# Pooled attention and a gated expert layer: batch 0's second half of k over SyncE's queue in fp32, and another order of the prologue's matmuls, copies and banks

## The chip, the cores and the metric

The kernel runs on one core of a Trainium2 chip. A core has five engines with instruction lists of their own: PE (TensorE, matrix multiplication; its weight loads are shown as PEld), DVE (VectorE), ACT (ScalarE), POOL (GpSimd) and SP (SyncE). They run side by side and wait for each other through semaphores. Data comes from HBM into SBUF by DMA. A DMA is issued by an engine, goes into that engine's queue and is worked off by 16 DMA engines that all queues share. Matmuls write into PSUM banks, and other engines copy the results from there.

The metric is the device time of one execution in microseconds, the median of several runs. Lower is better.

## The reference

```python
def _attn_ref(q, k, v) -> np.ndarray:
    B, H, S, D = q.shape          # 8, 8, 576, 64
    pool = 8
    Sp = S // pool                # 72
    scale = 1.0 / np.sqrt(D)
    k_p = k.reshape(B, H, Sp, pool, D).mean(axis=3)
    v_p = v.reshape(B, H, Sp, pool, D).mean(axis=3)
    scores = scale * np.matmul(q, k_p.transpose(0, 1, 3, 2))
    scores = scores - np.max(scores, axis=-1, keepdims=True)
    attn = np.exp(scores)
    attn = attn / (np.sum(attn, axis=-1, keepdims=True) + 1e-09)
    return np.matmul(attn, v_p).astype(np.float32)

def _moe_ref(x, w_in, w_out) -> np.ndarray:
    h = x @ w_in                  # 4608 x 512 by 512 x 2048
    g = h * np.cos(h)
    return (g @ w_out).astype(np.float32)
```

k and v are averaged over groups of eight positions, so that each head has 72 keys. The attention's output, 4608 tokens of 512 numbers, goes through two large matrix products with g = h cos(h) between them.

## The kernel before, in words

All matmuls are in bf16. The large products work on nine chunks of 512 tokens. For each chunk `up_mm` (L348) multiplies the tokens `xT` by the 16 column blocks of w_in, two blocks to a bank; ACT takes the cosine (L355), DVE multiplies (L358) and writes `g_sb`; `down_mm` (L361) multiplies by w_out and `down_out` stores the result. While PE works on chunk t, the attention of batch t + 1 is slipped between its matmuls. The attention of batch 0 has nothing to hide behind: it is the prologue, and the first L348 matmul can start only when it is done.

The order of the work is written out by hand: instructions stand on each engine in the order in which the code issues them, and an engine works its list off in order. An instruction that waits holds up everything behind it on its engine.

The prologue, by its lines:

- **Loads.** SyncE loads the first half of k (pairs of heads 0 and 1 of four) as fp32 into `k_first`, a piece of `g_sb` that is still free (L404). ACT and DVE each cast one pair to bf16 (`first_k`, L406). All other loads go over POOL's queue, which casts while it copies (`load_even`, L89): q's first half, k's second half, q's second half, v's halves, then the weights (L130, L135). Between the first two POOL computes three iotas (L413, L416), from which DVE makes `groups` (L427 to L431), the 0/1 matrix that sums groups of eight positions. POOL's later DMAs each wait for the landing of the DMA eight places ahead.
- **Warm-up.** `warm_up(n, bank)` (L472) runs n matmuls of a constant tile into a bank whose content nobody reads.
- **Pooled k.** `pool_k_mm` (L180) multiplies k by `groups`, 36 matmuls for two pairs, and hands back two closures that copy the result into `kk` (L186).
- **q transposed.** `q_transpose_mm` (L231) transposes nine blocks of q for each half; copies into `qT` follow (L232).
- **Scores.** `scores` multiplies q and pooled k (L251, eight matmuls for two units) and takes the exponential on ACT (L261) into `ex`. The list `us` has four units: token columns 0 to 255 and 256 to 511, each for heads 0 to 3 and heads 4 to 7. `REST` is the last 64 tokens for all heads.
- **Sums.** `sums_mm` (L280) sums `ex` over the keys; `inverse` makes 1/sum by Ln and Exp on ACT (L295, L296).
- **Pooled v.** `pool_v_mm` (L195), 18 matmuls for two pairs, and a copy into `vz` on DVE (L197).
- **Values.** `values_mm` (L289) multiplies `ex` by pooled v, `x_mul` (L303, DVE) multiplies by 1/sum and writes `xT`.

PSUM has three double banks (`banks[0..2]`) and two single ones (`obanks`). A step that writes a bank waits until the earlier reader of it is done, so the choice of banks is a choice of waits.

Of the kernel before, what the change touches and what calls it, by code (L numbers as in the profile page):

```python
# [9 lines left out]
FP32 = mybir.dt.float32  # L10
# [9 lines left out]
def kernel(  # L20
# [9 lines left out]
    nc = tc.nc  # L30
    B, H, S, D = q.shape
# [5 lines left out]
    KCH = d_model // 128  # L37
    FFCH = d_ff // 128
    NT = n_tokens // TILE
    ROW = S // 64  # L40
# [6 lines left out]
    REST = (SEG[2], (0, H))  # L47
# [17 lines left out]
    g_sb = wpool.tile([128, FFCH, TILE], BF16, name="g_sb")  # L65
# [11 lines left out]
    banks = [psum.tile([128, 2, 512], FP32, name=f"bank{i}") for i in range(3)]  # L77
    obanks = [psum.tile([128, 512], FP32, name=f"obank{i}") for i in range(2)]
# [6 lines left out]
    def even_view(src, b, j0=0, j1=KCH):  # L85
        return src[b, 2 * j0:2 * j1].rearrange("(j a) (p t) d -> (a p) j (t d)", a=2, t=ROW)

    def load_even(dst, b, src, j0=0, j1=KCH):
        nc.gpsimd.dma_start(out=dst[:, j0:j1].rearrange("p j t d -> p j (t d)"), in_=even_view(src, b, j0, j1))  # L89
# [100 lines left out]
    def pool_v_mm(b, pair, j0, j1):  # L190
        vb = staged["v", b]
        n = (j1 - j0) * D
        for t in range(ROW):
            for hp, rows in enumerate(half):
                nc.tensor.matmul(pair[:Sp, hp, 0:n], lhsT=groups[rows, t, :], rhs=vb[rows, j0:j1, t, :],  # L195
                                 start=(t == 0), stop=(t == ROW - 1))
        return lambda: nc.vector.tensor_copy(out=v_part(b)[:, j0:j1].rearrange("p j a d -> p a j d"),  # L197
                                             in_=pair[:Sp, :, 0:n].rearrange("p a (j d) -> p a j d", d=D))
# [26 lines left out]
    def q_transpose_mm(b, bank, g0, g1):  # L225

        if ("qT", b) not in att:
            qT_tile(b)
        ps = bank.bitcast(BF16)[:, 0:(g1 - g0) * 128].rearrange("p (g n) -> p g n", n=128)
        for g in range(g0, g1):  # L230
            nc.tensor.matmul(ps[:, g - g0, :], q_flat(b)[:, g * 128:(g + 1) * 128], identity, is_transpose=True)  # L231
        return lambda copy: copy(out=att["qT", b][:, g0:g1, :], in_=ps)  # L232
# [6 lines left out]
    def scores(b, u, pair):  # L239
        scores_mm(b, u, pair)  # L240
        scores_exp(b, u, pair)

    def scores_mm(b, u, pair):
        (c0, n), (h0, nh) = u

        for i in [i + 2 * a for k in range(0, nh, 4) for i in (k, k + 1) for a in range(2)]:
            bank, c = divmod(ex_col(u, i), nh * n // 2)
            pj, hp = divmod(h0 + i, 2)
            g, r = divmod(ROW * pj + ORDER[c0 // 64], 2)
            ps = pair[bank][:Sp, c:c + n] if isinstance(pair, tuple) else pair[:Sp, bank, c:c + n]  # L250
            nc.tensor.matmul(ps.rearrange("p (g n) -> p g n", n=64),  # L251
                             lhsT=kk[b % 2][half[r], h0 + i, 0:Sp],
                             rhs=att["qT", b][half[r], g:g + n // 64, hp * 64:hp * 64 + 64])
# [21 lines left out]
    def sums_mm(b, u, cs):  # L275

        ex = att["ex", b, u]
        q0 = u[1][0] // 4
        for i, q, rows, c in quads(u):
            nc.tensor.matmul(cs[rows, q - q0, :], lhsT=ones[:Sp, :], rhs=ex[:, c])  # L280

    def values_mm(b, u, ps):

        ex = att.pop(("ex", b, u))
        q0 = u[1][0] // 4
        for e in range(2):
            for i, q, rows, c in quads(u):
                pj, hp = divmod(u[1][0] + i, 2)
                nc.tensor.matmul(ps[rows, q - q0, e, :],  # L289
                                 lhsT=vz[b % 2][:, pj, 3 * hp, :].rearrange("p (d e) -> p e d", e=2)[:, e],  # L290
                                 rhs=ex[:, c])

    def inverse(cs, name, bufs):
        inv = asb.tile([128] + list(cs.shape[1:]), FP32, name=name, tag=name, bufs=bufs)
        nc.scalar.activation(out=inv, in_=cs, func=ACTF.Ln)  # L295
        nc.scalar.activation(out=inv, in_=inv, func=ACTF.Exp, scale=-1.0)  # L296
        return inv
# [102 lines left out]
    kv_even_tiles(0)  # L400
    q_tile(0)
    first_k = []
    k_first = g_sb.rearrange("p f n -> p (f n)").bitcast(FP32)[:, 0:2 * ROW * D]
    nc.sync.dma_start(out=k_first.rearrange("p (j n) -> p j n", j=2), in_=even_view(k, 0, 0, 2))  # L404
    for j, copy in enumerate((nc.scalar.copy, nc.vector.tensor_copy)):
        first_k.append(lambda j=j, copy=copy: copy(out=staged["k", 0][:, j].rearrange("p t d -> p (t d)"),  # L406
                                                   in_=k_first[:, j * ROW * D:(j + 1) * ROW * D]))
    first_k[0]()

    load_even(staged["q", 0], 0, q, 0, 2)  # L410
    row_of = consts.tile([128, ROW], FP32, name="row_of")
    for rows in half:
        nc.gpsimd.iota(row_of[rows], pattern=[[1, ROW]], base=0, channel_multiplier=ROW,  # L413
# [1 line left out]
    first_of = consts.tile([128, Sp], FP32, name="first_of")  # L415
    nc.gpsimd.iota(first_of, pattern=[[POOL, Sp]], base=0, channel_multiplier=0,  # L416
                   allow_small_or_imprecise_dtypes=True)
    load_even(staged["k", 0], 0, k, 2, 4)
    load_even(staged["q", 0], 0, q, 2, 4)
    load_even(staged["v", 0], 0, v, 0, 2)  # L420
    load_even(staged["v", 0], 0, v, 2, 4)
# [47 lines left out]
    def warm_up(n, bank):  # L469

        for i in range(n):
            nc.tensor.matmul(bank, lhsT=warm[:, 0:128], rhs=warm)  # L472
# [4 lines left out]
    def unit(bank):  # L477
        return bank.rearrange("p (q e n) -> p q e n", q=1, e=2)
# [2 lines left out]
    puts = pool_k_mm(0, obanks, 0, 2)  # L481
    puts[0](vec)
    puts[1](act)
    warm_up(3, banks[1][:, 0, :])
    puts = q_transpose_mm(0, banks[2][:, 0, :], 0, 5), q_transpose_mm(0, obanks[0], 5, 9)
    puts[0](vec)
    puts[1](act)
    warm_up(2, banks[1][:, 0, :])
    scores(0, us[0], banks[0])
    scores(0, us[1], banks[1])  # L490
    warm_up(1, banks[2][:, 1, :])
    for put in reversed(pool_k_mm(0, (obanks[1], obanks[0]), 2, 4)):
        put(vec)
    s01, s23 = (b_[:, 0, :].rearrange("p (i n) -> p i n", i=2) for b_ in banks[0:2])
    sums_mm(0, us[0], s01[:, 0:1])
    q_transpose_mm(0, banks[2][:, 0, :], 9, 14)(vec)
    sums_mm(0, us[1], s01[:, 1:2])
    q_transpose_mm(0, obanks[0], 14, 18)(vec)
    warm_up(1, banks[1][:, 1, :])
    inv01 = inverse(banks[0][:, 0, :], "inv", 1)  # L500
    put = pool_v_mm(0, banks[0], 0, 2)
    put()
    scores(0, us[2], banks[2])
    scores(0, us[3], banks[1])
    scores_mm(0, REST, tuple(obanks))
    for i in range(2):
        values_mm(0, us[i], unit(banks[0][:, i, :]))
    put = pool_v_mm(0, banks[2], 2, 4)
    for i in range(2):
        x_mul(0, 0, 256 * i, unit(banks[0][:, i, :]), inv01[:, 256 * i:256 * i + 256])  # L510
        if i == 0:
            put()
    for i in range(2):
        sums_mm(0, us[2 + i], s23[:, i:i + 1])
    for i in range(2):
        values_mm(0, us[2 + i], unit(banks[2][:, i, :]))
    for i in range(2):
        inv = inverse(s23[:, i, :], "inv_h", 2)
        x_mul(0, 1, 256 * i, unit(banks[2][:, i, :]), inv)
    scores_exp(0, REST, tuple(obanks))  # L520
    bk = banks
# [179 lines left out]
```

## Time and profile before

| what | value |
|---|---|
| median of 3 runs | 291.81 us (291.44 to 291.88) |
| profiled execution | 291.27 us |
| its span, first to last instruction | 289.4 us |
| PE busy | 282.8 us, 98% of the span |
| ACT / DVE / POOL busy | 142.2 / 170.0 / 146.1 us |
| first L348 matmul | at 15.97 us |
| DMA busy, first 24 us | 40 slices, nearly all at 9 tenths or more from 2.4 us on |

Times in the profile count from the first instruction. A line of the list by time has the start, the busy time, the engine, the line of code, the operation, what is written from what, the shape, the number of instructions merged into the line, and in brackets the idle time of the engine ahead of it and what ended it. The chain of waits is followed back from the last instruction: at each step to what released it.

### The profile page before, as it was taken

To read this page: it belongs to the slowest core of one execution; us is meant where nothing else is said; L and a number is where in the kernel's file an instruction comes from. 1 tells how busy PE (TensorE), PEld (TensorE's weight loads), DVE (VectorE), ACT (ScalarE), POOL (GpSimd) and SP (SyncE) were. 2 spreads that over 40 slices of the span, in tenths; PEclk is the share of its full clock that TensorE was granted. 3 is DMA by queue.
4 is the path that set the end of the run, shared out by engine and by line. 5 is a ranking of instruction groups with operands and counts; after the bars stand their busy time and mean duration, and the time that the engine had idled before them with its cause. 6 is when DMAs were issued, how large, how long until landed. Compare 5 with 4: busy or idle time off the path is not lost.

```text
span 289.4 us, 4940 instructions
## 1 busy us (share of the span) xinstructions
PE 282.8 (98%) x1993; PEld 147.3 (51%) x1993; DVE 170.0 (59%) x229; ACT 142.2 (49%) x142; POOL 146.1 (50%) x122
## 2 busy tenths in 40 slices
PE   7999999999999999999999999999999999999994
PEld 3655444555554555555555545554555454445444
DVE  5467885774757574658275737573666557216622
ACT  3786634678056904691369316840676066016400
POOL 8646937998974696479545982699000000000000
PEclk9999999999999999999999999999999999999998
DMA  7999999789977978795879866975703510230033
GB/s 142 202 204 211 205 208 197 143 164 190 167 147 102 203 114 169 101 169 110 166 74 200 120 139 119 179 139 108 140 1 73 120 39 0 49 82 16 0 72 74
DMA packets 57158, 36.59 MB, mean 126 GB/s; under 512 B 36400, under 2 KB 51184, under 8 KB 57136
## 3 DMA queue, kind: packets, MB, share of 16 engines
q0 software_dynamic: 17376, 18.06, 38.9%
q1 hardware_dynamic: 39520, 18.10, 32.3%
q8 instruction: 15, 0.25, 0.4%
q10 hardware_dynamic: 240, 0.13, 0.2%
q14 instruction: 7, 0.06, 0.1%
HBM read 36.70 MB, written 9.44 MB: 159 GB/s over the span
## 4 chain that ended last, share of the span: by engine, by line
PE 94%; DMA 2%; ACT 2%; issue 0%; DVE 0%; DVEq 0%; POOLq 0%
PE bank L348 43%; PE obank L361 27%; PE bank L361 8%; PE obank L367 5%; PE bank L251 3%; PE bank L320 3%; DMA q_b<-in_q_dram 2%; PE bank L367 2%; ACT ex L261 1%; PE bank L389 1%; PE bank L289 1%; PE bank L280 0%; PE bank L231 0%; PE obank L231 0%; PE bank L195 0%
## 5 line engine op out<-in xcount | busy, mean ns | idle before, releaser
L355 ACT ACTIVATE cos<-bank,half_pi 128x1024 f32<-128x1024 f32 x72 | 80.4, 1118 | 115.4 <-PE bank L348 115.4
L348 PE MATMUL bank<-xT,w_in_sb 128*128 128x512 bf16 x576 | 126.1, 379 | 0.0
L358 DVE TENSOR_TENSOR g_sb<-bank,cos 128x1024 bf16<-128x1024 f32 x72 | 88.1, 1224 | 48.9 <-ACT cos L355 48.8
L348 PEld LDWEIGHTS <-w_in_sb 128*128 128x128 bf16 x576 | 65.1, 113 | 59.2 <-issue 0.4
L361 PE MATMUL obank<-w_out_sb,g_sb 128*128 128x512 bf16 x360 | 83.9, 379 | 0.0
L361 PEld LDWEIGHTS <-g_sb 128*128 128x128 bf16 x462 | 42.0, 97 | 45.9 <-issue 2.0
L161 POOL TENSOR_TENSOR kv_st<-kv_st 72x2048 f32<-72x2048 bf16 (+1 forms) x13 | 50.4, 3875 | 16.9 <-DMA kv_st<-in_k_dram 16.8
L374 DVE COPY o_sb<-obank 128x512 f32<-128x512 f32 x21 | 14.4, 690 | 31.5 <-PE obank L361 28.6
L261 ACT ACTIVATE ex<-bank 72x1024 bf16<-72x1024 f32 x32 | 30.4, 1019 | 5.0 <-PE bank L251 5.0
L164 POOL TENSOR_TENSOR kv_st<-kv_st 72x1024 f32<-72x1024 f32 (+1 forms) x13 | 29.3, 2252 | 0.9
L361 PE MATMUL bank<-w_out_sb,g_sb 128*128 128x512 bf16 x102 | 27.6, 379 | 0.0
L324 DVE TENSOR_TENSOR x_r<-bank,inv_r 128x512 bf16<-128x512 f32 (+1 forms) x32 | 22.0, 689 | 1.1
L367 PE MATMUL obank<-w_out_sb,g_sb 64*128 64x512 bf16 x144 | 18.3, 376 | 0.0
L168 POOL TENSOR_TENSOR kp<-kv_st 72x512 bf16<-72x512 f32 (+1 forms) x14 | 16.1, 1169 | 0.5
L367 PEld LDWEIGHTS <-g_sb 64*128 64x128 bf16 x196 | 9.8, 94 | 7.3
L251 PE MATMUL bank<-qT,kk 64*72 64x256 bf16 (+1 forms) x184 | 13.2, 250 | 0.2
L251 PEld LDWEIGHTS <-kk 64*72 64x72 bf16 x192 | 8.4, 111 | 7.9 <-issue 3.4
L119 POOL DMA_DIRECT2D kv_st<-in_v_dram x15 | 9.7, 657 | 4.6 <-DVE vz L171 4.3
L320 PEld LDWEIGHTS <-ex 72*128 72x128 bf16 x192 | 8.7, 97 | 6.2 <-ACT ex L261 1.7
L321 DVE RECIPROCAL inv_r<-bank 128x8 f32<-128x8 f32 (+1 forms) x32 | 6.5, 203 | 8.2 <-PE bank L320 7.5
L529 POOL COPY gate<-kk 1x1 bf16<-1x1 bf16 x5 | 0.9, 178 | 20.4 <-DMA kk<-kp 20.4
L376 DVE COPY o_sb<-obank 128x512 f32<-128x512 f32 x6 | 4.1, 691 | 11.9 <-PE obank L367 11.9
(79 smaller groups left out, 167.3 us busy)
## 6 DMA issues: line engine op xcount, KB each, us to landing
out_dram<-o_sb SPq DMA_DIRECT2D x70, 128.0 KB, 2.4
q_b<-in_q_dram POOLq DMA_DIRECT2D x6, 576.0 KB, 8.8
kv_st<-in_k_dram POOLq DMA_DIRECT2D x6, 512.0 KB, 6.2
kv_st<-in_v_dram POOLq DMA_DIRECT2D x6, 512.0 KB, 10.1
w_in_sb<-in_moe_w_in_dram POOLq DMA_DIRECT2D x8, 256.0 KB, 10.8
w_out_sb<-in_moe_w_out_dram POOLq DMA_DIRECT2D x8, 256.0 KB, 10.0
q_b<-in_q_dram POOLq DMA_DIRECT2D x4, 288.0 KB, 8.4
kv_st<-in_k_dram POOLq DMA_DIRECT2D x3, 288.0 KB, 9.7
```

Of the source, the lines that this page charges most:

```text
L161: add(out=s, in0=x[:, :, 0:4, :], in1=x[:, :, 4:8, :], op=ADD)
L164: add(out=s[:, :, 0:2, :], in0=s[:, :, 0:2, :], in1=s[:, :, 2:4, :], op=ADD)
L168: add(out=kp[:, h0:h1, slot, :], in0=s[:, :, 0, :], in1=s[:, :, 1, :], op=ADD)
L251: nc.tensor.matmul(ps.rearrange("p (g n) -> p g n", n=64), lhsT=kk[b % 2][half[r], h0 + i, 0:Sp], rhs=att["qT", b][half[r], g:g + n // 64, ...
L261: nc.scalar.activation(out=ex[:, c:c + m * w].rearrange("p (a n) -> p a n", a=m), in_=src, func=ACTF.Exp, scale=scale / POOL)
L320: nc.tensor.matmul(out[:, o0:o0 + D + 1], lhsT=ex[:, c:c + 128], rhs=v1)
L324: nc.vector.tensor_mul(out=x[:m].rearrange("p e h d -> p h e d"), in0=vals, in1=scale_of)
L348: nc.tensor.matmul(h[:, j, :], lhsT=w_in_cols(ki, fc), rhs=xT[:, ki % 2, ki // 2, t * TILE:(t + 1) * TILE], start=(ki == 0), stop=(ki == K ...
L355: nc.scalar.activation(out=cos, in_=h, func=ACTF.Sin, bias=half_pi[:, :1])
L358: nc.vector.tensor_mul(out=g_sb[:, 2 * fp:2 * fp + 2, :], in0=h, in1=cos)
L361: nc.tensor.matmul(o, lhsT=g_sb[:, fc, ms * 128:(ms + 1) * 128], rhs=w_out_sb[fc // 4][:, fc % 4, :], start=(fc == 0), stop=(fc == FFCH - 1))
L367: nc.tensor.matmul(ps, lhsT=g_sb[rows, fc, ms * 128:(ms + 1) * 128], rhs=w_out_sb[fc // 4][rows, fc % 4, :], start=start, stop=stop)
```

## The change

The second half of k no longer goes over POOL's queue. SyncE loads it too, as fp32, in a second DMA, and DVE casts its two pairs. POOL's first DMA (q's first half) now comes behind the iotas. In the matmuls' order: the four q transposes that ACT copies come ahead of the five that DVE copies; q's second half is transposed in one go into the third double bank, ahead of both sums; the single warm-up matmuls (L491, L499) are gone; v's first half is pooled into another bank and its copy comes behind the scores of the third unit; the scores of REST come behind the first values; the sums of units 2 and 3 go into free columns of the single banks; both x products of the first heads come ahead of the copy of v's second half.

```diff
-    k_first = g_sb.rearrange("p f n -> p (f n)").bitcast(FP32)[:, 0:2 * ROW * D]
-    nc.sync.dma_start(out=k_first.rearrange("p (j n) -> p j n", j=2), in_=even_view(k, 0, 0, 2))
-    for j, copy in enumerate((nc.scalar.copy, nc.vector.tensor_copy)):
+    k_first = g_sb.rearrange("p f n -> p (f n)").bitcast(FP32)[:, 0:KCH * ROW * D]
+    for j in (0, 2):
+        nc.sync.dma_start(out=k_first.rearrange("p (j n) -> p j n", j=KCH)[:, j:j + 2], in_=even_view(k, 0, j, j + 2))
+    for j, copy in enumerate((nc.scalar.copy,) + (nc.vector.tensor_copy,) * 3):
...
-    load_even(staged["q", 0], 0, q, 0, 2)
     row_of = consts.tile([128, ROW], FP32, name="row_of")
...
-    load_even(staged["k", 0], 0, k, 2, 4)
+    load_even(staged["q", 0], 0, q, 0, 2)
     load_even(staged["q", 0], 0, q, 2, 4)
...
     puts[0](vec)
     puts[1](act)
+    first_k[2]()
+    first_k[3]()
     warm_up(3, banks[1][:, 0, :])
-    puts = q_transpose_mm(0, banks[2][:, 0, :], 0, 5), q_transpose_mm(0, obanks[0], 5, 9)
-    puts[0](vec)
-    puts[1](act)
+    q_transpose_mm(0, obanks[0], 5, 9)(act)
+    q_transpose_mm(0, banks[2][:, 0, :], 0, 5)(vec)
     warm_up(2, banks[1][:, 0, :])
     scores(0, us[0], banks[0])
     scores(0, us[1], banks[1])
-    warm_up(1, banks[2][:, 1, :])
     for put in reversed(pool_k_mm(0, (obanks[1], obanks[0]), 2, 4)):
         put(vec)
-    s01, s23 = (b_[:, 0, :].rearrange("p (i n) -> p i n", i=2) for b_ in banks[0:2])
-    sums_mm(0, us[0], s01[:, 0:1])
-    q_transpose_mm(0, banks[2][:, 0, :], 9, 14)(vec)
-    sums_mm(0, us[1], s01[:, 1:2])
-    q_transpose_mm(0, obanks[0], 14, 18)(vec)
-    warm_up(1, banks[1][:, 1, :])
+    puts = q_transpose_mm(0, banks[2][:, 0, :], 9, 14), q_transpose_mm(0, banks[2][:, 1, :], 14, 18)
+    for put in puts:
+        put(vec)
+    s01 = banks[0][:, 0, :].rearrange("p (i n) -> p i n", i=2)
+    for i in range(2):
+        sums_mm(0, us[i], s01[:, i:i + 1])
     inv01 = inverse(banks[0][:, 0, :], "inv", 1)
-    put = pool_v_mm(0, banks[0], 0, 2)
+    put = pool_v_mm(0, banks[1], 0, 2)
+    scores(0, us[2], banks[2])
     put()
-    scores(0, us[2], banks[2])
     scores(0, us[3], banks[1])
-    scores_mm(0, REST, tuple(obanks))
     for i in range(2):
         values_mm(0, us[i], unit(banks[0][:, i, :]))
+    scores_mm(0, REST, tuple(obanks))
+    s23 = [ob[:, 256:512] for ob in obanks]
+    sums_mm(0, us[2], s23[0].unsqueeze(1))
     put = pool_v_mm(0, banks[2], 2, 4)
     for i in range(2):
         x_mul(0, 0, 256 * i, unit(banks[0][:, i, :]), inv01[:, 256 * i:256 * i + 256])
-        if i == 0:
-            put()
-    for i in range(2):
-        sums_mm(0, us[2 + i], s23[:, i:i + 1])
+    put()
+    sums_mm(0, us[3], s23[1].unsqueeze(1))
     for i in range(2):
         values_mm(0, us[2 + i], unit(banks[2][:, i, :]))
     for i in range(2):
-        inv = inverse(s23[:, i, :], "inv_h", 2)
+        inv = inverse(s23[i], "inv_h", 2)
         x_mul(0, 1, 256 * i, unit(banks[2][:, i, :]), inv)
```

## The prediction

> **What bounds the kernel now.** I read the chain of waits for the first 30 us, then the busy time by stretch, then the list of instructions in order of time up to 24 us, and last the DMA queues in narrow windows. The stretches and the chain first (start, length, what):
>
> ```profile
> 15.97:60.00 44.03, 43.88 (x281) 22.51 (x278) 31.63 (x40) 27.02 (x29) 31.32 (x34) 1.00 1.09 193
> ...
> 60.00:120.00 60.00, 60.00 (x432) 31.41 (x430) 36.56 (x50) 31.24 (x31) 46.25 (x33) 1.00 0.89 150
> ...
> 1.26 6.02 DMA q_b<-in_q_dram
> ...
> 9.09 1.94 ACT ex L261 x2
> ...
> 13.03 1.94 ACT ex L261 x2
> ...
> 15.41 0.58 PE bank L289 x16
> 16.00 12.36 PE bank L348 x56
> ```
>
> From 15.97 us on, PE (first pair of numbers after the length) has no gap worth naming: 43.88 of 44.03 us, then 60.00 of 60.00. Whatever delays the first L348 matmul delays the end by as much, and nothing later gives it back. So the change is priced by one number: when L348 starts. Before that, the chain runs through q's first half (issued 1.26, landed 7.28), its transposes, two exponentials, two more, and the second product with v. The instructions that hang on it:
>
> ```profile
> 7.33 0.45 PE L231 MATMUL bank<-identity,q_b 128*128 128x128 bf16 x5 [0.36 <-DMA q_b<-in_q_dram]
> ...
> 7.82 0.49 DVE L232 COPY qT<-bank 128x640 bf16<-128x640 bf16 x1 [0.96 <-PE bank L231]
> ...
> 9.09 1.93 ACT L261 ACTIVATE ex<-bank 72x1024 bf16<-72x1024 f32 x2 [0.46 <-PE bank L251]
> ...
> 10.41 1.30 DVE L186 CAST kk<-obank 64x144 bf16<-64x144 f32 x4 [2.10 <-PE obank L180]
> ...
> 14.08 0.69 DVE L303 TENSOR_TENSOR xT<-bank,inv 128x512 bf16<-128x512 f32 x1 [0.80 <-ACT ex L261]
> ```
>
> The queues in the windows 1.8 to 3.7 us and 3.7 to 7.3 us (packets, MB, share of 16 engines):
>
> ```profile
> q1 hardware_dynamic: 247, 0.56, 88.7%
> ...
> q0 software_dynamic: 408, 0.45, 99.9%
> ```
>
> Until 3.7 us only SyncE's transfer of k's first half moves. q's first half, whose issue on POOL was over at 2.15, has moved nothing: it stands behind it. Then POOL's queue moves 0.45 MB in 3.6 us (125 GB/s) although, once running, its transfers land 1.45 us apart (q 7.28, k 8.7, q 10.2, v 11.6, by issue time plus time to landing), which for 0.29 MB is 200 GB/s. It starts slowly.
>
> **The change part by part.** The sum is made against the profiled execution: span 289.4, time 291.27, so 1.87 us lie around the span. The median of the three runs, 291.81, is 0.54 above it, and I add differences to the median.
>
> *k's second half goes to SyncE's queue.* It takes a 0.76 us issue from POOL and gives SyncE a second one of 0.47, right behind the first, so at about 1.7. From 2.6 to 3.6 us the first half moves at about 390 GB/s; the second, 0.59 MB, takes 1.49 us more of all engines. It now stands ahead of q's first half, which is on the chain. This is the decisive term and no row shows two such transfers together. Upper end: q lands 1.49 later, 8.77, with its slow start unchanged. Lower end: the slow start is over by the time that k is through (3.9 + 1.49 = 5.4), so 1.45 for the data and 0.4 to be seen (k's first half ended at 3.9 and its copy started at 4.32): 7.25. I take 8.4. The nearest row is this same transfer behind the same neighbour, which is the upper end; a part of the slow start should be used by k's own packets. That POOL's queue starts slowly whenever it has been idle is seen again after 61.8 us, where 1.0 us passes at under 60 GB/s. Term: +1.12, between -0.03 and +1.49.
>
> [...] The row: two SyncE stores of 128 KB issued at 68.4 and 68.9 us, while POOL's queue was full, landed 5.8 us after issue against 2.4 over all stores; so a queue waits for much of what the other has in hand. [...]
>
> *q's issue moves behind three iotas.* They took from 2.15 to 2.81, so the issue starts up to 0.66 later, or hardly later if they fit into POOL's idle 0.81 us ahead of 1.26. As long as q stands behind k anyway, this is hidden by k's transfer; counted 0. The pooling matrix (DVE L427 to L431, now from 2.90 to 5.32) comes up to 0.9 earlier, but the pooling of k also needs ACT's copy, done at 4.99, and PE's ten warm-up matmuls, done at 5.27; it starts at 5.37 now. At most 0.1, and q is later still: 0. q's second half, v and the weights are issued some 0.7 earlier and one transfer less stands ahead of them. They wait for nothing new: w_in's first part, now 15.7 (6.36 + 9.3), lands 7.0 after q instead of 8.4, so at 15.4, ahead of the new start of L348. POOL's waits for an earlier transfer's landing stay, each one transfer earlier.
>
> *Two more casts on DVE.* 0.44 each by the DVE row of L406. They stand in DVE's list behind the copies of kk (done 6.87) and ahead of the copy of q's transposes, so they wait for k's second half and the copy, and every score, waits for them. If k lands by 7.3 they end by 8.2; the nine transposes end 0.75 after q's landing, at 9.15. Hidden: 0. It costs when k lands late.
>
> *Transposes in another order.* ACT's four go first, DVE's five last. Now landing to first exponential is 9.09 - 7.28 = 1.81. After: 0.77 to the end of nine transposes, 0.49 copy, 0.06 to PE, 0.45 for four scores (12.56 to 13.01 in the chain): 1.77. Term: -0.04.
>
> *From the first exponential (T) to L348.* Now 15.97 - 9.09 = 6.88. The single warm-up after the scores (0.39) is gone: pooling ends at T+0.9, DVE's four copies of kk (1.30) at T+2.3, both copies of qT (0.49, 0.41, in one bank pair, their transposes already done) at T+3.15 instead of T+3.47. ACT: two exponentials, sums, Ln and Exp (0.60, 0.63) are through at T+3.58, so the next two run T+3.62 to T+5.55 instead of T+3.94 to T+5.88. That is 0.33 won on ACT. But DVE: v's copy (0.42) ends T+3.60, the four scores that wait for its bank and the 16 products (0.62) end T+4.54, then both x products (0.69, 0.68) run T+4.66 to T+6.01 with v's second copy behind them instead of between them: T+6.40. The last 16 products start at T+6.46, L348 at T+7.05. Loss 0.17. Against it, now the ninth L348 matmul (15.97 + 8 x 0.216 = 17.70) waits for the last x product (17.74 and 0.06 to PE), 0.1; after, that product ends at T+8.57 and the matmul is due at T+8.78. Term: +0.07. If DVE's order did not bind, the end would go by ACT: T+5.55, sums 0.3, products 0.59, so T+6.45, 0.53 better than now's 6.98 with its wait; if DVE's waits cost 0.1 at three places, +0.4. Between -0.5 and +0.4.
>
> Sum: 1.12 - 0.04 + 0.07 = **+1.15**, so 291.81 + 1.15 = 292.96, about 293.0.
>
> **The rivals.**
> 1. *q goes first, k's second half last.* For it: q's issue is over long before 3.7 even when 0.66 later. Against it: k's second half is in the engines' hands from about 2.4. Then k lands at 8.7 as now, DVE's two casts end at 9.65, copy 0.49, 0.06, scores 0.45: T = 10.67, 1.58 later, +0.07: 293.5.
> 2. *The slow start is hidden.* q lands at 7.0 to 7.4 behind k because its queue was ready and waiting. Against it: now, too, it waited (2.15 to 3.7) and was slow nevertheless. T is then 8.8 to 9.2: -0.25 to +0.15, so 291.6 to 292.0, no change.
> 3. *Faster.* One mechanism, at DVE's x products: v's second copy is in time, so that ACT's chain sets L348's start at T+6.45, worth 0.53 against now. It decides only if q lands before 7.3; from 7.85 on q's delay has eaten it. With q at 7.2: -0.08 - 0.04 - 0.53 = -0.65, 291.2. Against it: 1.35 us of x products stand ahead of the copy.
> 4. *PE's clock.* Two warm-ups fewer, and PE idles from 7.0 to about 8.4. The granted clock is 1.00 in every stretch but the last; a loss for some 3 us of L348 at half rate would be +1.5 more. The idle stretch is short; little chance.
>
> **How the numbers follow.** Forecast 0.45, rival 1 0.20, rival 2 0.22, rival 3 0.07, rival 4 0.04, and 0.02 for the rest. About 0.2% (0.58 us) is what a measurement of this kernel can tell from no change: 291.23 to 292.39. Faster holds rival 3: 0.07. Same: rival 2 and the 0.08 of the forecast in which q lands before 7.8: 0.30. Slower: the rest, 0.63. The forecast's own range is 292.2 to 293.4 (q from 7.65 to 8.8). The whole: from 291.4 (rival 2 with 0.2 won after T) to 293.7 (rival 1 and 0.2 lost after T).
>
> **What would show it.** In the changed kernel's list by time: L231 waits for q's DMA until 8.1 to 8.8; DVE's casts L407 end before the transposes do; first L261 1.77 after q's landing; third L261 3.6 after the first; two L303 back to back at T+4.7 with L197 behind them and L289 waiting for it; L348 at about 17.2. Wrong: q landing by 7.4, or L407 starting after 8 us (rival 1), or L348 less than 6.7 after T.

## The result, and the profile after

| | before | after |
|---|---|---|
| median of eight runs each | 291.59 us (291.42 to 291.88) | 292.48 us (292.33 to 292.82) |
| profiled execution, its span | 291.27, 289.4 us | 292.54, 290.5 us |
| q's first half issued, landed | 1.26, 7.28 us | 1.41, 8.35 us |
| k's second half landed | 8.71 us | 5.81 us |
| v's first half landed | 11.59 us | 11.26 us |
| first exponential (T) | 9.09 us | 10.10 us |
| first L348 matmul | 15.97 us, with the wait of its ninth 16.07 | 16.90 us, by the ones behind it 16.93 |
| first of the last group of matmuls, L389, in the chain of waits | 282.00 us | 282.83 us |

The changed kernel is slower by 0.89 us: ratio 1.0031, 95% interval 1.002 to 1.0042. The forecast was 293.0 with a range from 291.4 to 293.7, slower.

First the stretches of after (length, busy us and count for PE, PEld, DVE, ACT and POOL, then the granted clock, the DMA share and GB/s):

```profile
16.93:60.00 43.07, 42.92 (x277) 22.05 (x274) 30.84 (x40) 25.34 (x26) 30.08 (x32) 1.00 1.14 191
60.00:120.00 60.00, 60.00 (x432) 31.40 (x430) 36.72 (x50) 31.76 (x31) 45.45 (x32) 1.00 0.85 148
```

From the first L348 matmul on, PE has no gap here either, and the delay passes through: +0.86 at L348, +0.83 at L389. What changed lies ahead of 17 us, or behind the last matmul.

The instructions of after that answer to those shown of before, from the list by time:

```profile
7.52 0.88 DVE L407 CAST kv_st<-g_sb 128x576 bf16<-128x576 f32 x2
8.39 0.51 PEld L231 LDWEIGHTS <-q_b 128*128 128x128 bf16 x9 [1.29 <-DMA q_b<-in_q_dram]
...
9.11 0.49 DVE L232 COPY qT<-bank 128x640 bf16<-128x640 bf16 x1 [0.71 <-PE bank L231]
10.10 1.93 ACT L261 ACTIVATE ex<-bank 72x1024 bf16<-72x1024 f32 x2 [0.69 <-PE bank L251]
...
12.30 0.69 PE L195 MATMUL bank<-kv_st,groups 64*72 64x128 bf16 x18
...
14.68 1.29 DVE L303 TENSOR_TENSOR xT<-bank,inv 128x512 bf16<-128x512 f32 x2 [1.14 <-PE bank L289]
15.88 0.41 DVE L197 CAST vz<-bank 72x256 bf16<-72x256 f32 x1
```

The transposes still wait for q's DMA, now until 8.39. DVE's two new casts end at 8.40, and the copy behind them waits for PE until 9.11, so they hold up nothing here. (The chain of waits of after leads through these casts, because they end within 0.05 us of q's landing. But PE's own wait for DVE ahead of the transposes was over at 7.58, while what it waited for after that, q, came at 8.35.) Both x products stand back to back, with v's second copy behind them.

The queues of after in the windows 1.8 to 5.2 and 5.2 to 8.4 us (packets, MB, share of 16 engines):

```profile
q1 hardware_dynamic: 525, 1.16, 95.9%
q0 software_dynamic: 2, 0.00, 1.3%
```

```profile
q0 software_dynamic: 438, 0.49, 106.7%
```

Until 5.2 us both halves of k move on SyncE's queue (q1) and nothing of q (q0). The engines were kept from q for 1.5 us longer, as the change's size said, and q landed 1.07 later.

The other place is the very end. These are the waits of SyncE after 284 us, before and then after (engine, line, what was waited for: us in total, times, longest):

```profile
SPq L696 <- DMA out_dram<-o_sb: 1.2, 1, 1.2
```

```profile
SPq L696 <- DMA out_dram<-o_sb: 1.5, 1, 1.5
```

When the last store is issued, SyncE goes through a list of waits for the landings of stores, and the kernel ends behind it. This took 0.27 us longer: from the end of the last weight load of L389 to the last instruction 4.05 us before and 4.33 after.

So the profiled executions differ by 0.83 at L389 and 0.27 behind it, 1.1 in all, as their spans do (289.4 and 290.5). Their times differ by more, 1.27, because time less span is 1.86 us before and 2.02 after. That holds beyond the two profiles: it is 2.0 to 2.15 us in the eight runs of after, and 1.86 on average in the 98 runs of before that were taken beside the experiments. So some 0.2 us of the loss lies outside the span, where no profile shows what it is. The medians differ by only 0.89, because the profiled execution of before, 291.27, is below its median and that of after, 292.54, above; the runs below show what varies.

### The profile page after: what moved, and what is told of

The parts are those of the page before. It is cut to its first block, busy times and chain, and to the rows that moved or that the text cites. A ratio compares the mean times of both kernels' runs of the same rounds, so it can differ in the third digit from the quotient of the medians.

```text
span 290.5 us, 4941 instructions
## 1 busy us (share of the span) xinstructions
PE 282.9 (97%) x1991; PEld 147.1 (51%) x1991; DVE 170.6 (59%) x231; ACT 142.0 (49%) x142; POOL 145.5 (50%) x121
## 4 chain that ended last, share of the span: by engine, by line
PE 95%; DVE 2%; ACT 1%; issue 0%; DVEq 0%
PE bank L348 43%; PE obank L361 27%; PE bank L361 8%; PE obank L367 5%; PE bank L251 3%; PE bank L320 3%; PE bank L367 2%; PE bank L472 2%; PE bank L389 1%; PE bank L289 1%; ACT ex L261 1%; DVE qT L232 0%; DVE xT L303 0%; PE obank L180 0%; DVE kv_st L407 0%; PE obank L231 0%
## 5 line engine op out<-in xcount | busy, mean ns | idle before, releaser
L348 PE MATMUL bank<-xT,w_in_sb 128*128 128x512 bf16 x576 | 126.0, 379 | 0.0
L348 PEld LDWEIGHTS <-w_in_sb 128*128 128x128 bf16 x576 | 65.1, 113 | 59.1 <-issue 0.2
```

Of the source, the lines that this page charges most:

```text
L348: nc.tensor.matmul(h[:, j, :], lhsT=w_in_cols(ki, fc), rhs=xT[:, ki % 2, ki // 2, t * TILE:(t + 1) * TILE], start=(ki == 0), stop=(ki == K ...
```

## The experiments

Twelve kernels ran, in four groups; each group was measured against runs of before taken with it (medians 291.43, 291.43, 291.43 and 291.54 us). The table has what each profile gives. T is the first exponential, "T to L348" runs to the first L348 matmul, worked back by 0.216 us per matmul where a later one had to wait or the first has no record. The tail runs from the end of the last weight load of L389 to the last instruction. "Clock full" is when TensorE's granted clock became full in that execution; until then the warm-up matmuls start 0.43 us apart, and the L348 matmuls behind it 0.216 (before).

| kernel | median us | ratio (95%) | clock full | q landed | v landed, after T | T | T to L348 | tail |
|---|---|---|---|---|---|---|---|---|
| before, first profile | 291.59 | | 4.48 | 7.28 | 2.50 | 9.09 | 6.98 | 4.05 |
| after | 292.48 | 1.0031 (1.002 to 1.0042) | 6.35 | 8.35 | 1.16 | 10.10 | 6.83 | 4.33 |
| order_only | 291.85 | 1.0017 (1.0008 to 1.0025) | 7.33 | 7.26 | 1.99 | 9.62 | 6.83 | 4.06 |
| loads_only | 292.66 | 1.0039 (1.0027 to 1.0051) | 7.27 | 7.72 | 1.39 | 9.67 | 6.98 | 4.30 |
| q_issue_first | 291.98 | 1.0019 (1.001 to 1.0027) | 7.27 | 8.24 | 1.49 | 9.99 | 6.83 | 4.31 |
| no_second_k | 291.33 | 0.9996 (0.9986 to 1.0005) | 6.55 | 6.50 | 0.66 | 9.41 | 6.83 | 4.06 |
| before_again | 291.51 | 1.0004 (0.9995 to 1.0012) | 7.19 | 7.23 | 2.69 | 9.52 | 6.98 | 4.05 |
| order_only_again | 291.76 | 1.0012 (1.0004 to 1.0021) | 7.37 | 7.26 | 2.33 | 9.62 | 6.98 | 4.03 |
| prime | 292.04 | 1.0021 (1.0005 to 1.0037) | 6.60 | 7.91 | 1.06 | 9.66 | 6.83 | 4.31 |
| q_on_sync | 292.20 | 1.0025 (1.0015 to 1.0035) | 4.19 | 5.92 | 1.98 | 8.91 | 6.83 | 4.33 |
| late_half | 291.81 | 1.0014 (1.0005 to 1.0022) | 4.67 | 7.36 | 2.89 | 9.17 | 7.53 | 4.05 |
| no_three | 291.45 | 0.9999 (0.999 to 1.0008) | 7.27 | 7.62 | 2.64 | 9.43 | 6.98 | 4.07 |
| prime_new | 292.52 | 1.0049 (1.0032 to 1.0066) | 4.90 | 7.15 | 3.39 | 8.96 | 8.37 | 4.05 |
| k_second_late | 299.31 | 1.0267 (1.0218 to 1.0316) | 7.01 | 8.02 | 2.62 | 9.77 | 11.37 | 4.33 |

### One part of the change alone

**order_only** keeps the loads of before and takes the new order from the transposes on.

```diff
 (against before: loads unchanged)
-    puts = q_transpose_mm(0, banks[2][:, 0, :], 0, 5), q_transpose_mm(0, obanks[0], 5, 9)
-    puts[0](vec)
-    puts[1](act)
+    q_transpose_mm(0, obanks[0], 5, 9)(act)
+    q_transpose_mm(0, banks[2][:, 0, :], 0, 5)(vec)
...
+    put = pool_v_mm(0, banks[1], 0, 2)
+    scores(0, us[2], banks[2])
     put()
...
```

> The loads of the kernel before with the changed order of matmuls, copies and banks alone. If the delay of q's first half is the whole cost and the order is a small gain: q lands at 7.3 us, the first exponential starts at 9.05, the first large matmul at about 15.9 (6.8 later), time 0.1 to 0.2 us below the kernel before. If the order itself costs: 0.3 us or more above it. If the order is worth the 0.5 us that ACT's chain alone would allow: 0.5 below.

**loads_only** does the opposite: the new loads, the old order, DVE's two new casts where the change has them.

```diff
 (against before; SyncE's two transfers as in the change)
...
-    load_even(staged["k", 0], 0, k, 2, 4)
+    load_even(staged["q", 0], 0, q, 0, 2)
...
     puts[1](act)
+    first_k[2]()
+    first_k[3]()
     warm_up(3, banks[1][:, 0, :])
```

> The changed loads (k's second half on SyncE's queue, q's issue behind the iotas, two casts on DVE) with the old order of matmuls, copies and banks. If q's late landing is the cost: q lands at about 8.35, first exponential 1.8 later at 10.15, first large matmul at 17.0, time 1.0 to 1.1 us above the kernel before. If the order was the cost: within 0.3 us of the kernel before.

Both are slower than before, by some 0.4 and 1.2 us, and so the loss belongs to the loads and the order gives none of it back by itself. The profiles say more. With the old order T to L348 is 6.98 us, with the new one 6.83, so the new order does gain 0.15 here. It was lost again in the median of order_only, which I could not yet explain.

The profiled execution of loads_only, 292.06, is its shortest. In it q landed at 7.72, but DVE's copy of its transposes came only at the end of the two casts, 8.77. From the chain of waits, and then from the list by time:

```profile
1.47 4.45 PE bank L472 x10
5.92 1.26 PE obank L180 x36
...
7.82 0.95 DVE kv_st L407 x2
8.77 0.41 DVE qT L232
```

```profile
7.80 0.44 PE L231 MATMUL bank<-identity,q_b 128*128 128x128 bf16 x5
...
8.51 0.58 ACT L232 COPY qT<-obank 128x512 bf16<-128x512 bf16 x1 [0.74 <-PE obank L231]
```

The ten warm-up matmuls end at 5.92 and not at 5.27 as in the profile of before, everything that DVE does with k comes later, and the two casts stand in the way of the copy: the five transposes that it reads were done at 8.24, so it came some 0.4 us late. The scores also need ACT's copy, which ended at 9.09, and DVE's ended at 9.17; so the casts cost T about 0.1, by estimate from these two ends. The prediction called these casts hidden. In after they are, with 0.7 us to spare, and here they are not.

**q_issue_first** is after with q's issue ahead of the iotas again.

```diff
+    load_even(staged["q", 0], 0, q, 0, 2)
     row_of = consts.tile([128, ROW], FP32, name="row_of")
...
-    load_even(staged["q", 0], 0, q, 0, 2)
     load_even(staged["q", 0], 0, q, 2, 4)
```

> The changed kernel with one thing undone: POOL issues q's first half ahead of the three iotas again, at 1.3 instead of 1.4 us. If q stands behind k's second half in the engines whatever its issue: q lands within 0.2 us of 8.35 and the time is within 0.2 us of the changed kernel's. If each engine took turns between the queues and q only just missed its turn: q lands near 7.3 and k's second half near 8.7, and DVE's casts then hold up the copy: T later than 10.4, time 0.4 us above the changed kernel.

q is issued at 1.26, k's second half at 1.28, and yet q landed at 8.24 and k at 6.03. POOL's place for the issue is not what matters; being issued first does not put q first. This ends rival 1. Its median was 0.55 above before, less than after's 0.89; the two were not measured side by side, and q's landing, 0.11 earlier, explains only a part of the difference. The rest stays open.

**no_second_k** is after without SyncE's second transfer; the two casts read the first half again.

```diff
-    for j in (0, 2):
+    for j in (0,):
...
-                                                   in_=k_first[:, j * ROW * D:(j + 1) * ROW * D]))
+                                                   in_=k_first[:, j % 2 * ROW * D:(j % 2 + 1) * ROW * D]))
```

> The changed kernel without SyncE's second DMA: the second half of k is not loaded at all, and DVE's two casts read the first half again, so that the output is not the reference's. It takes away the transfer and leaves the casts. If the transfer ahead of q is the cost: q lands at 7.3, and the casts, which end at 7.8 to 8.4, are then the last to release the copy of q's transposes; first exponential at 9.1 to 9.4, time 0.6 to 1.0 us below the changed kernel. If the casts on DVE are the cost: no change.

Without this one transfer all of the loss is gone: 291.33 against 291.43. q landed at 6.50, 1.85 earlier than in after. T moved by only 0.69, since the copy now waits for something else: PE's warm-up matmuls end at 7.68 in this execution, its transposes at 8.38, and DVE's casts ("7.61 0.86 DVE kv_st L407 x2" in its chain) at 8.47. And the tail is 4.06 again, not 4.33.

### What one execution differs by from another

**before_again** and **order_only_again** are the same kernels once more, for their profiles.

> The kernel before, unchanged, to see how much one profiled execution differs from the next: PE's clock became full at 4.5 us in the first profile and at 6.4 to 7.3 us in the five others. If the clock's time is chance and PE's warm-up and pooling then hold the transposes: with the clock full after 6.5 us, transposes at 7.8 to 8.0 whatever q's landing, first exponential at 9.6, first large matmul at 16.5, span 289.8. If only q's landing counts: first exponential at 9.1 at any clock. The time is that of the kernel before within 0.15 us.

> The old loads with the changed order once more, because its median (0.42 us above the kernel before) went against its profile, in which the stretch from the first exponential to the first large matmul was 6.83 us against 6.98. If the order is the loss: again 0.3 to 0.5 us above, and a profile in which v's first half, landing at 11.6, is waited for by the pooling of v, which the changed order reaches 2.2 us after the first exponential instead of 3.0. If the first time was chance: within 0.2 us of the kernel before.

The chain of waits of before_again, where that of before had q's DMA until 7.28:

```profile
1.47 4.45 PE bank L472 x10
5.92 1.22 PE obank L180 x36
7.13 0.80 PE bank L472 x3
7.93 0.28 PE bank L231 x5
```

q landed at 7.23, but PE was busy with warm-up matmuls until 7.93. In this execution TensorE's clock became full at 7.19 us, in the first profile of before at 4.48. That moved T from 9.09 to 9.52 in the same kernel, and the time from 291.27 to 291.66. The runs without a profile point the same way. Of the 98 runs of before beside the experiments, the 30 with a mean clock of 0.997 or 0.998 (0.997 in the first profile) have a median of 291.26 us, and the 51 with 1.000 (as in before_again) one of 291.52. Over the fourteen profiles the clock became full between 4.19 and 7.37 us. So the kernel before is not always bound by q's landing, as the prediction took it to be; in one of its two profiles it was PE.

For order_only the two profiles differ behind T. The first has 6.83 to L348, the second 6.98. In the second v's first half landed at 11.95, and its pooling (L195) started at 11.99, right behind; in the first it landed at 11.61 and the pooling started at 11.83, when PE came to it. The new order comes to this pooling 2.2 us after T.

**late_half** tells the front part of the order from the rest: transposes as before, and the new order only behind the pooling of k's second half.

```diff
 (against order_only)
-    q_transpose_mm(0, obanks[0], 5, 9)(act)
-    q_transpose_mm(0, banks[2][:, 0, :], 0, 5)(vec)
+    puts = q_transpose_mm(0, banks[2][:, 0, :], 0, 5), q_transpose_mm(0, obanks[0], 5, 9)
+    puts[0](vec)
+    puts[1](act)
```

> Loads as before, the first transposes, their banks and the two plus three warm-ups as before; from the pooling of k's second half on, the order after the change (transposes of q's second half ahead of the sums, v's pooling in another bank and later, the sums of the third and fourth units in the upper halves of the other banks, two single warm-ups gone). Theory: what order_only loses (ratios 1.0017 and 1.0012, some 0.3 to 0.4 us) is, first, 0.10 us up to the first exponential, because the copy that the first scores wait for now reads transposes that PE does last (9.62 against 9.52 in executions where TensorE's clock became full at 7.2 to 7.4 us), and second, a wait for v's first half: from the first exponential to L348 it takes 6.83 us where v's pooling starts 2.2 us after that exponential, and 6.98 where the pooling had to wait for v's landing (11.95 us in order_only_again), more where the clock is early. Then late_half keeps only the second: 291.35 to 291.65 us, first exponential at 9.5 (late clock) or 9.1 (early). Rival: the loss lies in the late part as a whole (the warm-ups removed there, or its banks): 291.7 to 291.9, as order_only.

It came out as order_only, at 291.81, just above my upper end, so the median alone spoke for the rival, that the late part loses as a whole. Its profile has a clock that was full early, T at 9.17, and this, from the list by time:

```profile
10.63 0.68 PE L231 MATMUL bank<-identity,q_b 128*128 128x128 bf16 x9 [0.58 <-DMA q_b<-in_q_dram]
11.24 0.40 PE L280 MATMUL bank<-ex,ones 72*32 72x256 bf16 x8
12.10 0.69 PE L195 MATMUL bank<-kv_st,groups 64*72 64x128 bf16 x18 [0.46 <-DMA kv_st<-in_v_dram]
```

PE waits for q's second half and then for v's first half, and T to L348 is 7.53. The four profiles of the new order with v's first half in question fit one line: L195 starts at T+2.20 in after, T+2.21 in order_only, T+2.37 in order_only_again and T+2.93 in late_half, and L348 follows 4.6 us behind in each (4.63, 4.62, 4.61, 4.60). The old order came to the pooling only at T+2.97 (12.49 in before_again), so v had 0.8 us more time. With the loads of before v lands 2.0 to 2.9 us after T. With those of after it lands at T+1.16, and the new order has its gain. The order's gain is 0.15 if v is early, and a loss of up to 0.55 if v is late. This is the late part's loss, and the rival's other causes (the missing warm-ups, the banks) aren't needed for it, though no run took them alone.

**no_three** is before without the three warm-up matmuls ahead of the transposes.

```diff
-    warm_up(3, banks[1][:, 0, :])
     puts = q_transpose_mm(0, banks[2][:, 0, :], 0, 5), q_transpose_mm(0, obanks[0], 5, 9)
```

> The kernel before without the three warm-up matmuls between the pooling of k and the first transposes. Theory: in executions where TensorE's clock becomes full only at 6.3 to 7.4 us these three matmuls end at 7.93 us, 0.65 us after q's first half has landed (7.25), and the transposes wait for PE, not for q. Without them the transposes start at 7.3 whatever the clock: first exponential at 9.05 to 9.15 instead of 9.52 in such an execution, unchanged at 9.09 where the clock is early; median 291.1 to 291.35 us (ratio about 0.9993), and less spread. Rival: the three matmuls keep the clock; without them the idle 1 us ahead of the transposes puts the clock's full grant off, and the time is 0.3 us or more longer (291.8 and above).

No difference: 291.45 against 291.43. PE was free at 7.14, but in this execution q landed at 7.62, so T was 9.43. The gain that I expected isn't shown, and neither is the rival's loss. What the three matmuls cost in the median is within the interval, under 0.3 us either way.

### Who goes first in the DMA engines

**prime** adds to after a load of 128 x 16 elements on POOL's queue, ahead of q.

```diff
+    prime = consts.tile([128, 16], BF16, name="prime")
+    nc.gpsimd.dma_start(out=prime, in_=q[0, 0, 0:128, 0:16])
```

> The changed kernel with one more small load (128 pieces of 16 numbers, read by nobody) on POOL's queue ahead of q's first half. If the slow start of POOL's queue is paid by whatever comes first: q lands 0.5 to 1.0 us earlier than 8.35 although it is issued 0.6 later, and the time falls by 0.2 to 0.6 us. If the slow start comes with q's own data or with k's traffic beside it: q lands at 8.35 or later and the time is the changed kernel's or 0.2 us more.

q was issued 0.92 later than in after (2.33) and landed 0.44 earlier (7.91). The bytes moved in 40 slices of the first 8 us, after and then prime:

```profile
GB/s 0 0 0 0 0 0 0 0 0 127 127 219 242 346 403 415 403 415 392 392 426 415 403 380 380 334 138 92 98 121 132 161 167 190 184 202 190 173 179 138
```

```profile
GB/s 0 0 0 0 0 0 0 0 0 138 184 265 403 392 438 392 346 380 415 426 403 380 415 438 323 224 222 209 196 202 179 167 167 161 144 138 179 202 144 179
```

In after there is a hole of about 1 us behind k, at 92 to 138 GB/s, before POOL's queue reaches its 160 to 200. In prime there is none right behind k (196 to 224 GB/s there). So the slow start was still on the path in after, as the prediction took it to be, and part of it can be hidden behind SyncE's transfer.

**prime_new** carries this over to the loads of before, with late_half's order and without the three warm-up matmuls.

```diff
 (against late_half)
+    prime = consts.tile([128, 16], BF16, name="prime")
+    nc.gpsimd.dma_start(out=prime, in_=q[0, 0, 0:128, 0:16])
     load_even(staged["q", 0], 0, q, 0, 2)
...
-    warm_up(3, banks[1][:, 0, :])
```

> late_half, without the three warm-up matmuls, and with a load of 128 x 16 elements of q on POOL's queue ahead of q's first half. Theory: POOL's queue starts slowly after idling, at about 60 to 100 GB/s for its first microsecond against 160 to 190 later, and the small load takes that start beside k's transfer on SyncE's queue: behind k's second half it brought q's landing from 8.35 to 7.91 although q was issued 0.9 us later. With only k's first half ahead, q lands at 6.3 to 6.9 (7.28 before), the first exponential is at 8.2 to 8.7, v's first half lands at about 11 (2.3 to 2.8 us after the first exponential, so the 6.83 us to L348 become 6.9 to 7.3): 290.8 to 291.3 us. Rival: the small load costs POOL 0.9 us of issuing and gains nothing where the queue is idle anyway: q lands at 7.3 or later, v's halves 0.9 us later, and the time is 291.5 to 292.2.

The theory fell: q landed at 7.15, no earlier to speak of than the 7.23 to 7.62 in the profiles with before's loads and no small load, though the small load itself had landed at 4.42. v's second half was late on top, 15.43, and held the pooling (L195 at 15.48), which made T to L348 8.37. The rows of this run show the hole again behind k (93 and 86 GB/s at 3.8 to 4.2 us). Why the small load helps behind two transfers of SyncE's and not behind one stays open.

**q_on_sync** asks what happens if the transfer that gains from SyncE's queue is q's: q's first half goes behind k's first half on SyncE, cast by ACT and DVE, and k's second half goes on POOL as before.

```diff
-    for j in (0, 2):
...
+    for j, src in ((0, k), (2, q)):
+        nc.sync.dma_start(out=k_first.rearrange("p (j n) -> p j n", j=KCH)[:, j:j + 2], in_=even_view(src, 0, 0, 2))
...
-    load_even(staged["q", 0], 0, q, 0, 2)
+    load_even(staged["k", 0], 0, k, 2, 4)
```

> The changed kernel with the two loads exchanged: q's first half goes over SyncE's queue in fp32 behind k's first half, and ACT and DVE cast one pair each; k's second half goes first on POOL's queue. If the landing of q's first half sets the prologue: q lands at 5.8, is cast by about 8.1 (behind the copies of kk), k's second half lands at 8.3, the first exponential comes at 9.4 to 9.9 and the time is 0.2 to 0.7 us below the changed kernel. If k's second half then holds up the rest: pooling of the second half waits until 8.4 only, so no. If the copies on ACT and DVE are the limit: as the changed kernel.

SyncE's second transfer, now q's, landed at 5.92, and in the profiled execution (clock full at 4.19) T was 8.91, the earliest of all, and the time 291.28, as the profile of before. The median, 292.2, is not better: its runs spread from 291.28 to 292.51. Its profile shows casts on ACT and DVE between k's copies and q's transposes, so T hangs on when PE gives them k; that this makes the longer times is an argument, since no such execution was profiled. The runs' clocks fit it: the two with a mean clock of 0.997 took 291.28 and 291.39 us, the four with 1.000 took 292.38 to 292.47.

**k_second_late** lets k's second half go last, as rival 1 would have it: its transfer writes a place that the first cast has read, so it cannot be issued earlier.

```diff
-    for j in (0, 2):
-        nc.sync.dma_start(out=k_first.rearrange("p (j n) -> p j n", j=KCH)[:, j:j + 2], in_=even_view(k, 0, j, j + 2))
+    nc.sync.dma_start(out=slots[:, 0:2], in_=even_view(k, 0, 0, 2))
...
     first_k[0]()
+    nc.sync.dma_start(out=slots[:, 0:3:2], in_=even_view(k, 0, 2, 4))
...
-    first_k[2]()
-    first_k[3]()
...
     q_transpose_mm(0, banks[2][:, 0, :], 0, 5)(vec)
+    first_k[2]()
+    first_k[3]()
```

> After, but SyncE's second transfer of k goes into a place that the cast of k's first sixteenth-size piece must have read first, so it can start only at about 5.3 us (that cast ended at 5.2 in the profiles), when q's first half is already under way; the two further casts stand behind the copy of q's transposes on VectorE. Theory: all that the change costs is k's second half ahead of q; with q alone behind k's first half, q lands at 7.0 to 7.9 (7.28 before; 8.35 after), the first exponential is at 9.1 to 9.7, v's first half lands at 10.4 to 11.2, ahead of its pooling, and L348 is 6.83 us behind the first exponential: 291.1 to 291.8 us. Rival: the transfers share the engines at once, q's slower ones lose, and q lands at 8.3 or later again: 292.2 to 292.8. A second rival: k's second half lands later than 9.3, its pooling holds the scores of the third unit, and q's early landing gains nothing: 292 or more with an early first exponential.

The second rival held, by more than I had thought. q landed at 8.02, later than the 7.0 to 7.9 of the theory, and k's second half only at 12.83. From the chain, the DMA and what waits for it, and PE's list:

```profile
4.91 7.92 DMA g_sb<-in_k_dram
12.83 0.03 issue
12.85 0.47 DVE kv_st L407
```

```profile
13.37 1.13 PE L180 MATMUL obank<-groups,kv_st 64*64 64x72 bf16 x36 [3.42 <-DVE kv_st L407]
```

The same 0.59 MB that took until 5.81 when issued at 1.28 took 7.9 us when issued at 4.91, beside POOL's transfers. PE waited 3.4 us for it, and its clock fell: the 36 pooling matmuls took 1.13 us against 0.77 in other profiles, and the mean granted clock over the execution was 0.992. The profiled execution, 296.77 us, is one of the two shortest; three of the six took 300.8 with a mean clock of 0.974, and none of those was profiled.

None of the kernels was faster than before. One thing was not tried: the new loads with a second transfer on a queue other than SyncE's, which might leave the tail alone.

## Why the prediction was right, point by point

**What bounds the kernel.** Right for the path behind L348: +0.86 there, +0.83 at L389. Two things were missing. Whether q's landing is ahead of PE depends on when TensorE's clock becomes full (4.48 us in the first profile of before, 7.19 in before_again), which one profile cannot tell: in before_again PE held the transposes, and T was 0.43 later than in the profile that I worked from. And the end was priced by L348 alone, though something behind the last matmul could change as well, and so could the time outside the span.

**"q lands at 8.4", +1.12.** It landed at 8.35, +1.07. The choice near the upper bound was right, and so was its reason, that the slow start of POOL's queue is used only in part by k's own transfer: the hole behind k (92 to 138 GB/s) is still there in after and gone in prime. no_second_k, which drops only this transfer, brings q back by 1.85, and with it the whole loss. q's first half did not come between k's two: it landed at 8.35 behind k's 5.81 in after, and at 8.24 behind 6.03 in q_issue_first. Only when SyncE's second transfer was issued 3.6 us later (4.91 against 1.28), in k_second_late, did it have to share the engines: between 4.9 and 13 us POOL's queue moved 1.21 MB and SyncE's 0.59.

**The iotas, 0.** Right: they fitted into POOL's idle time ahead of its first DMA, so q's issue moved by 0.15, and q_issue_first, which takes that back, has q still behind k.

**Two more casts on DVE, hidden: 0.** Right in after: they end at 8.40 where the prediction had 8.2, since the pooling started at 5.85 and not 5.37, and DVE then has nothing to do until the copy at 9.11. In loads_only, where q landed at 7.72, the copy waited for them.

**The order of the transposes, -0.04.** Landing to T took 1.75 against 1.81, so -0.06; forecast 1.77.

**From T to L348, +0.07.** This is the term that was mis-sized: it measured -0.15 (6.83 against 6.98), in after and in five more profiles. The step is "both x products T+4.66 to T+6.01", with v's second copy behind them. They started at T+4.58, and the copy behind them started 1.20 later, not 1.35, because DVE's instructions overlap in part (the two x products take 1.29 together in the list above, and the copy starts at 15.88, before their end at 15.97); so the copy started at T+5.78, and the last 16 products at T+6.25 and not T+6.46. The ninth matmul's wait is gone, as forecast. That v's landing can hold this stretch was not seen; it doesn't in after, by 1.0 us (landed 11.26, pooled at 12.30), but it does with the loads of before.

**What the sum left out: the end, +0.27.** Six kernels have a second transfer on SyncE's queue, and their tails are 4.30 to 4.33; eight have not, and theirs are 4.03 to 4.07. no_second_k differs from after by that transfer alone. The first of SyncE's last waits for stores came through 2.37 us behind the start of the last L389 matmul before, and 2.64 after, and seven more waits, 0.06 to 0.09 us apart but for one step of 0.4, stand behind it in both. SyncE's last store lands 1.8 us after its issue and ACT's 2.1. The semaphores in the traces tell which store that first wait is for: before, SyncE's own last one (landed at 2.35), with the wait for ACT's at the end of the list; after, ACT's (landed at 2.63). So SyncE now meets the later of the two first, and the other seven waits come behind it. It is so in all six kernels with the second transfer and in none of the eight without. Why one more DMA near the start changes which store the list begins with is not shown.

**The sum.** Term by term the profiles give 1.07 - 0.06 - 0.15 + 0.27 = 1.13, against the 1.15 of the forecast. That it came so close is luck: two errors cancelled, -0.22 after T and +0.27 at the end. The forecast also kept the 1.87 us around the span as they were, and they became 2.02. The measured median difference is 0.89, since in the profile of before the clock became full early. Taken against before_again, L348 is later by 0.43 (16.93 and 16.50), the end of the span by 0.70, and the time by 0.88 (292.54 and 291.66), of which 0.17 lie outside the span; against the first profile the time is longer by 1.27. The medians' 0.89 is near the first of these. And the forecast added its sum to 291.81, 0.22 above the median of the later runs.

**The rivals.** Rival 1, q first, is refuted by q_issue_first. Rival 2, q at 7.0 to 7.4, by its 8.35; the chance of 0.22 for it was reasonable, as prime shows that it takes little to hide part of the slow start. Rival 3's mechanism exists, but DVE still binds: T to L348 is 6.83 and not 6.45. Rival 4: the clock did not fall in after (1.00 in each stretch above), so two warm-ups fewer cost nothing that a profile shows. Half rate for some 3 us, as its estimate has it, is what the start of before shows: 0.43 us per warm-up matmul against 0.216 for L348, over the 3.0 us from 1.47 to 4.48.

## What to carry to other kernels

When a transfer is moved to a faster queue (here from POOL's, at 160 to 200 GB/s once running, to SyncE's, at about 400), look at what it now stands in front of: here it arrived 2.9 us earlier, where nothing waited for it, and it pushed back by 1.1 us the one transfer that everything waited for. An order of work has its due dates for data, and a better order with earlier dates can lose with the old loads and win with the new, so try the two parts separately and together. Before you price a prologue from one profile, take a second: one start-up state can make another engine the bound (here PE in place of q's DMA, with the clock full at 7.19 us and not at 4.48).

## What the runs showed that I had not expected

- One more DMA on SyncE near the start makes the end longer by 0.27 us, in six profiles of six: SyncE's list of final waits then begins with the store that lands last.
- The time outside the span is not a constant: 1.86 us before, 2.02 in the profile of after. It is 1.93 in that of no_second_k, which has no second transfer, and 1.85 in that of loads_only, which has it, so the transfer alone does not make it; the cause stays open.
- TensorE's clock became full anywhere between 4.19 and 7.37 us, with the first warm-up matmul always at about 1.47. That is a spread of 3.2 us, from 2.7 to 5.9 us behind that matmul, and no run shows what sets the point. Between the two profiles of before (4.48 and 7.19) it moved the warm-up's end from 5.27 to 5.92, and T by 0.43.
- One transfer of 0.59 MB on SyncE's queue landed 4.5 us after its issue when it was issued 0.1 us ahead of POOL's, and 7.9 us after it when POOL's queue was already moving.
